# Spatial mixing of an attention and gMLP block in 26 block products instead of 28, on one Trainium2 core

## The chip, the cores and the metric

The kernel runs on one core of a Trainium2 chip. A core has five engines with queues of their own, which run in order and meet only at semaphores: TensorE (PE, matrix products, with its weight loads shown as PEld), VectorE (DVE), ScalarE (ACT), GpSimd (POOL) and SyncE (SP), which here only issues DMAs. SBUF is the working memory with 128 partitions, PSUM holds eight banks of 128 x 512 float32 into which TensorE accumulates. The metric is the device time in microseconds (us) of one execution; the median of several runs counts.

## What is computed

A block of a transformer with 2048 rows and 448 columns in float32: layer norm with a modulation from a condition vector, 16-head attention, then a second layer norm with modulation and a gated MLP whose gate mixes the rows. The part that the change touches most is the second half:

```python
z = _gelu(jnp.einsum("bsd,df->bsf", x, w_in))
z1 = z[..., :Fh]
z2 = _layernorm(z[..., Fh:], axis=-1)
g = jnp.einsum("ts,bsf->btf", w_sp, z2) + b_sp[None, :, None]
return jnp.einsum("bsf,fd->bsd", z1 * g, w_out)
```

Fh is 896, so g is the product of a 2048 x 2048 matrix w_sp with the 2048 x 896 matrix z2. This is the spatial mixing.

## The kernel before

Precision. TensorE works on float32r operands, a rounded float32. To come near float32 the kernel splits an operand into a high part (rounded) and a low part (the rest) and does three products: high by high, high by low, low by high. A split is a copy on ScalarE (`act.activation(hi, raw, AF.Copy)`) and a subtraction on VectorE (`sub`, line 82). So each 128 x 128 by 128 x 512 block costs three matmuls (lines 1262 to 1264, in `mix_step`) and needs both operands split.

Order of the work. The schedule is written by hand: instructions go to each engine's queue in program order. First the projections; then attention (lines 790 to 900), a loop over 256 slots, 16 to a head: per slot four score products (`s_mm`), four products for the running maximum (`m_mm`) of a head 20 slots ahead, and the value products (`pv_mm`). A table of events hangs further work on slots: at a head's slot of the maximum, `m_max` reduces on VectorE and then does three small operations on GpSimd, and `m_fin` transposes the result on TensorE and writes it by DMA into the query tile. Then the output projection, the first half of the gated MLP (`z1_unit`, stored to `z1_scr`), the second half (`z2_gemm` and `z2_norm`, 16 row tiles), the mixing, and the output product (`y_part`).

Sums of weight blocks. The mixing uses a fast matrix product in which blocks of w_sp are added or subtracted before they are multiplied. These sums depend on the weights only; they are made during attention. `ws_load(i)` fetches two 128 x 512 blocks into one of three pairs of buffers, `ws_add(i)` combines them on GpSimd (line 804), `ws_store(i)` writes the result to `ws_scr`. They sit on slots j, j + 3 and j + 5; there are 80 (five sums of 16 blocks) between slots 2 and 190. SP issues all these DMAs in order, so that a load waits until the store three sums before has landed.

Mixing. w_sp is cut into 2 x 2 blocks, z2 into two halves of rows and its first six channel tiles of 128 into two groups of three (`F1`, `F2`); the seventh tile (`F6`) is computed without the fast product along with them. That makes seven products of 2 x 2 block schemes, each four quarter-size blocks long: 28 block products of 2 x 4 by 4 x 4 blocks for the six tiles. They run in four phases of two halves of eight steps (`PHASES`, `steps`). A step loads the weight block or blocks (`w_load`), splits them (`w_split`), and does three matmuls for each of seven (last phase: four) channel tiles. At the end of each half `evac` adds seven accumulators into the four quarter results `u11` to `u22`. Sums of z2 for later phases are made on GpSimd (`z_sum`), the split stationary operands by `prep0` to `prep3`. `gate` adds the bias and multiplies by z1, `u_split` splits the result for the output product. The first four output tiles run inside the last phase, the other twelve behind it.

Of the kernel before, what the change touches and what calls it, by code (L numbers as in the profile page):

```python
# [31 lines left out]

@with_exitstack
def tile_adaln_mha_gmlp(ctx, tc, x, wqkv, wo, w_in, w_spT, b_sp, w_out, cT, w_mod0, w_mod, out):
# [13 lines left out]
    ws_scr = scr.tile([80, 128, 512], F32, name="ws_scr")  # L48
# [572 lines left out]
    ppool = att.enter_context(tc.tile_pool(name="ppool", bufs=6))  # L621

# [148 lines left out]
    def win_first(i):  # L771
# [6 lines left out]
    SUMS = (  # L778
        ((0, 1), (1, 1), ALU.subtract),
        ((1, 0), (0, 0), ALU.subtract),  # L780
        ((0, 0), (1, 1), ALU.add),
        ((0, 0), (0, 1), ALU.add),
        ((1, 0), (1, 1), ALU.add),
    )

    def w_block(rc, st, half):
        rb, cb = rc
        return w_spT[(rb * 8 + st) * 128 : (rb * 8 + st + 1) * 128, (2 * cb + half) * 512 : (2 * cb + half + 1) * 512]

    ws_raw = []  # L790

    def ws_tiles(i):
        if not ws_raw:
            ws_raw.append(dpool.tile([128, 7, 512], F32, name="ws_raw", tag="heapF"))
        return [ws_raw[0][:, 2 * (i % 3) + j, :] for j in range(2)]

    def ws_load(i):
        k, j = divmod(i, 16)
        for t, rc in zip(ws_tiles(i), SUMS[k]):
            sp.dma_start(t, w_block(rc, j // 2, j % 2))  # L800

    def ws_add(i):
        a, b = ws_tiles(i)
        pool.tensor_tensor(out=a, in0=a, in1=b, op=SUMS[i // 16][2])  # L804

    def ws_store(i):
        sp.dma_start(ws_scr[i], ws_tiles(i)[0])
# [315 lines left out]
    F1, F2, F6, FQ = slice(0, 384), slice(384, 768), slice(768, 896), slice(384, 896)  # L1123

    PHASES = (("s", 0, (1, 1)), ("s", 1, (0, 0)), ("s", 2, 3), ("s", 4, None))
    steps = [(p, half, st) for p in range(4) for half in range(2) for st in range(8)]

    def w_sources(p, half, st):
        _, k, q = PHASES[p]
        res = [ws_scr[k * 16 + st * 2 + half]]  # L1130
        if q is not None:
            res.append(ws_scr[q * 16 + st * 2 + half] if isinstance(q, int) else w_block(q, st, half))
        return res[::-1] if p == 3 else res
# [3 lines left out]
    def w_load(n):  # L1137
        if n < len(steps) and n not in raws and n not in wsp:
            raws[n] = []
            for src in w_sources(*steps[n]):  # L1140
                t = wp.tile([128, 512], F32, name="raw_sp")
                sp.dma_start(t, src)
                raws[n].append(t)

    def w_split(n):
        if n < len(steps) and n not in wsp:
            wsp[n] = []
            for raw in raws.pop(n):
                hi = wp.tile([128, 512], F32R, name="wsp_h")
                act.activation(hi, raw, AF.Copy)  # L1150
                lo = wp.tile([128, 512], F32R, name="wsp_l")
                sub(dve, lo, raw, hi)
                wsp[n].append((hi, lo))

    def z_sum(dst, a, b, op=ALU.add, eng=pool):
        eng.tensor_tensor(out=dst, in0=a, in1=b, op=op)

    def z_part(hi, lo, src):
        act.activation(hi, src, AF.Copy)
        sub(dve, lo, src, hi)  # L1160

    def prep0(st):
# [10 lines left out]
    def prep2(st):  # L1173
        z_part(zst[st][:, 0:896], zst[st][:, 896:1792], z2[st])
# [30 lines left out]
    for t in range(NT + 1):  # L1205
# [6 lines left out]
        if t in (13, 15):  # L1212
            w_split(t // 15)
# [305 lines left out]
```

## Time and profile before

| what | value |
|---|---|
| time, median of 3 runs | 1396.1 us (1394.71 to 1397.45) |
| the profiled execution: its time | 1395.53 us |
| the profiled execution: its span, first to last instruction | 1393.7 us |
| granted TensorE clock | 1.0 |
| attention, first score product to last value product | 145.1 to 866 us |
| z2 products | 977.9 to 1049.3 us |
| mixing with four output tiles | 1049.3 to 1336.9 us |
| remaining output tiles | 1336.9 us to the end |

How to read the lines below. In the groups of instructions a row gives the line of the kernel, engine, operation, output and inputs by the program's names, shapes, and the count; then total busy time and the mean duration of one in ns; then how long the engine was idle before them and what ended that wait. In the timeline a row begins with the start and the duration in us. Matmuls are pipelined, so that their durations overlap. A line can be that of a helper: line 82 is every subtraction of a split. "x12" behind a row counts the instructions merged into it.

### The profile page before, as it was taken

The page shows a single profiled execution, that of the slowest core. Times are in us where ns is not written, and L with a number is a line of the kernel's source. Part 1 is how long each engine was busy: PE and PEld are TensorE (multiplying, and loading weights), DVE is VectorE, ACT ScalarE, POOL GpSimd, SP SyncE. Part 2 cuts the span into 40 slices and gives each one's busy share as a digit, 9 for nine tenths or more (in the row PEclk, how much of TensorE's full clock was granted, in tenths as well). Part 3 has the DMA queues.
Part 4 walks back from the last instruction along what each step waited for, and adds up shares of the span by engine and source line. Part 5 has one row for each costly group of instructions (what it writes and reads, how often), then busy time and mean ns, then how long its engine had stood idle before and what let it go on. Part 6 is the DMA issues. An engine that isn't in the chain of part 4 may idle for free.

```text
span 1393.7 us, 20308 instructions
## 1 busy us (share of the span) xinstructions
PE 1388.7 (100%) x7170; PEld 987.0 (71%) x7170; DVE 1033.3 (74%) x1770; ACT 782.4 (56%) x1498; POOL 278.9 (20%) x279
## 2 busy tenths in 40 slices
PE   9999999999999999999999999999999999999998
PEld 8888655555555555555555555988998888888888
DVE  7898888888888888888888850850477655668574
ACT  6623677666667777777777779363234544434211
POOL 2144212222224143323200021100132330000000
PEclk9999999999999999999999999999999999999999
DMA  8465644655466556555323001534103333445453
GB/s 294 139 168 181 184 116 154 172 167 164 148 172 167 161 165 190 158 161 155 108 68 78 20 18 50 187 119 140 46 6 109 113 111 110 143 138 164 141 174 110
DMA packets 99633, 187.01 MB, mean 134 GB/s; under 512 B 17672, under 2 KB 29578, under 8 KB 96986
## 3 DMA queue, kind: packets, MB, share of 16 engines
q1 hardware_dynamic: 96814, 181.54, 43.2%
q10 hardware_dynamic: 2718, 4.19, 0.8%
q8 instruction: 56, 0.92, 0.3%
q14 instruction: 45, 0.37, 0.1%
HBM read 130.42 MB, written 50.46 MB: 130 GB/s over the span
## 4 chain that ended last, share of the span: by engine, by line
PE 99%; DVE 1%; DMA 0%; issue 0%; POOL 0%; ACTq 0%; DVEq 0%
PE st_ps L671 19%; PE o_ps L686 17%; PE mt L639 17%; PE acc L1262 7%; PE acc L1264 7%; PE acc L1263 7%; PE z_ps L1188 5%; PE pq L335 5%; PE z_ps L1074 5%; PE wo_ps L761 3%; PE pv L317 2%; PE y_ps L1369 2%; PE y_ps L1370 2%; PE y_ps L1368 2%; PE tp L111 1%; PE pv L464 0%
## 5 line engine op out<-in xcount | busy, mean ns | idle before, releaser
L644 DVE TENSOR_REDUCE pm<-mt 128x1 f32<-128x512 f32 x1024 | 631.0, 683 | 86.6 <-PE mt L639 86.6
L675 ACT ACTIVATE P<-st_ps 128x512 f32<-128x512 f32 x1024 | 516.4, 628 | 202.4 <-PE st_ps L671 201.6
L671 PE MATMUL st_ps<-qst,kst 128*128 128x512 f32 x1024 | 406.1, 406 | 0.0
L639 PE MATMUL mt<-kst,qst 128*128 128x512 f32 x1024 | 402.9, 393 | 0.0
L671 PEld LDWEIGHTS st_ps<-qst,kst 128*128 128x128 f32 x1024 | 191.1, 187 | 141.0 <-issue 93.1
L686 PE MATMUL o_ps<-P,V 128*32 128x512 f32 x2048 | 246.2, 598 | 0.0
L639 PEld LDWEIGHTS mt<-kst,qst 128*128 128x128 f32 x1024 | 192.4, 188 | 32.3
L804 POOL TENSOR_TENSOR ws_raw<-ws_raw 128x512 f32<-128x512 f32 x80 | 103.2, 1290 | 292.9 <-DMA ws_raw<-in_w_spT_dram 292.8
L1150 ACT ACTIVATE wsp_h<-raw_sp 128x512 fp32r<-128x512 f32 x112 | 70.2, 633 | 153.1 <-PE acc L1264 102.0
L82 DVE TENSOR_TENSOR wsp_l<-raw_sp,wsp_h 128x512 fp32r<-128x512 f32 x112 | 82.1, 742 | 81.1 <-ACT wsp_h L1150 80.4
L686 PEld LDWEIGHTS o_ps<-P,V 128*32 128x32 f32 x2048 | 53.5, 109 | 123.0 <-issue 117.7
L1262 PE MATMUL acc<-wsp_h,heapA 128*128 128x512 f32 x224 | 87.3, 390 | 0.0
L1263 PE MATMUL acc<-wsp_l,heapA 128*128 128x512 f32 x224 | 87.2, 389 | 0.0
L1264 PE MATMUL acc<-wsp_h,heapA 128*128 128x512 f32 x224 | 87.2, 389 | 0.0
L1263 PE MATMUL acc<-wsp_l,heapB 128*128 128x512 f32 x174 | 67.7, 389 | 0.0
L1264 PE MATMUL acc<-wsp_h,heapB 128*128 128x512 f32 x174 | 67.7, 389 | 0.0
L1262 PE MATMUL acc<-wsp_h,heapB 128*128 128x512 f32 x174 | 67.7, 389 | 0.0
L335 PE MATMUL pq<-heapD,heapD 128*128 128x512 f32 x196 | 61.9, 390 | 0.0
L1192 DVE BATCH_NORM_STATS2 stz<-z 128x6 f32<-128x448 f32 x32 | 19.8, 624 | 44.3 <-ACT z L1191 23.4
L1264 PEld LDWEIGHTS acc<-wsp_h,heapA 128*128 128x128 f32 x224 | 42.1, 188 | 8.8
L1262 PEld LDWEIGHTS acc<-wsp_h,heapA 128*128 128x128 f32 x224 | 42.0, 188 | 8.8 <-DVE cD L1268 0.3
L1263 PEld LDWEIGHTS acc<-wsp_l,heapA 128*128 128x128 f32 x224 | 42.1, 188 | 8.6
(225 smaller groups left out, 1600.5 us busy)
## 6 DMA issues: line engine op xcount, KB each, us to landing
ws_raw<-in_w_spT_dram SPq DMA_DIRECT2D x160, 256.0 KB
ws_scr<-ws_raw SPq DMA_DIRECT2D x80, 256.0 KB
raw_sp<-ws_scr SPq DMA_DIRECT2D x80, 256.0 KB
kst<-qk_scr SPq DMA_DIRECT2D x45, 224.0 KB
qst<-qk_scr SPq DMA_DIRECT2D x45, 224.0 KB
raw_sp<-in_w_spT_dram SPq DMA_DIRECT2D x32, 256.0 KB
qk_scr<-qh SPq DMA_DIRECT2D x28, 256.0 KB
qk_scr<-ql SPq DMA_DIRECT2D x28, 256.0 KB
```

Source lines behind the costliest of these rows:

```text
L82: eng.tensor_tensor(out=dst, in0=a, in1=hi.bitcast(F32), op=ALU.subtract)
L335: pe.matmul(pq, wqk[:, b, m * 128 : (m + 1) * 128], hT[g][:, a, :], start=j == 0, stop=j == NST - 1)
L639: pe.matmul(mt, qst[h % 3][:, t * 128 : (t + 1) * 128], kst[h % 3][:, kb * 512 : (kb + 1) * 512], start=True, stop=True)
L644: dve.tensor_reduce(out=pms[h][:, t, kb : kb + 1], in_=mt, axis=AX.X, op=ALU.max)
L671: pe.matmul(st, kst[h % 3][:, kt * 128 : (kt + 1) * 128], qst[h % 3][:, qb * 512 : (qb + 1) * 512], start=True, stop=True)
L675: act.activation(p, st, AF.Exp, scale=SCALE)
L686: pe.matmul(otile[h][32 * qb : 32 * qb + 32, :], V[:, kt, h, :], ptiles.pop((u, qb)), start=kt == 0, stop=kt == NT - 1)
L804: pool.tensor_tensor(out=a, in0=a, in1=b, op=SUMS[i // 16][2])
L1150: act.activation(hi, raw, AF.Copy)
L1262: pe.matmul(acc[i], zh, hi, start=st == 0, stop=False)
L1263: pe.matmul(acc[i], zh, lo, start=False, stop=False)
L1264: pe.matmul(acc[i], zl, hi, start=False, stop=st == 7)
```

## The change

The six channel tiles are now mixed in 26 block products. w_sp is used as a 4 x 4 arrangement of 512 x 512 blocks, z2 as 4 row groups by two channel groups. Each product p of `MIX` names the sums of z blocks to make first (`z_sum`, on GpSimd), the z operand and its sign, the weight operand (a stored sum, or a plain block), and which results take the accumulator's value after it. Two sets of three PSUM banks alternate between products, and they are never cleared: after product p the bank holds the sum over p, p - 2, p - 4 and so on, and `evac` adds or subtracts that running sum in the result.

In attention there are now 28 sums instead of five (each of four blocks, 112 sums of 128 x 512 instead of 80), some of sums made before; they take slots 2 to 243. For the 22 sums that are operands, two of four blocks also get their low part here, by a copy and a subtraction on GpSimd, and a second store to `wl_scr`. The mixing then loads these low parts in place of computing them; the other low parts of the 26 products are made on GpSimd.

Channel tile 6 is mixed in plain form: 64 block steps of three matmuls, spread over the steps of the products by `F6_AT` (12 of the 64 reuse a weight block that the product has loaded anyway). Its accumulator is one PSUM bank for a result at a time. The bias enters with the first eviction, so that `gate` is one operation. The four first output tiles run behind the mixing with the others. The reserved scratch for DMA descriptors is cut to 4096.

```diff
+W_SUMS = (
+    ((3, 3), (3, 1), -1),
...
+    (4, 11, -1),
...
+MIX = (
+    (((T0, 4, 7, 1), (T1, 0, T0, 1)), T1, 1, 6, ((1, 1, -1), (1, 3, -1))),
+    ((), T0, 1, 2, ((1, 0, 1),)),
+    (((ONCE, 3, T1, 1),), ONCE, 1, 3, ((0, 2, 1),)),
+    (((T1, 1, 2, 1), (ONCE, T1, T0, -1)), ONCE, 1, 11, ((0, 0, -1),)),
...
 def ws_add(i):
+    v, kt = divmod(i, 4)
     a, b = ws_tiles(i)
-    pool.tensor_tensor(out=a, in0=a, in1=b, op=SUMS[i // 16][2])
+    pool.tensor_tensor(out=a, in0=a, in1=b, op=ALU.add if W_SUMS[v][2] > 0 else ALU.subtract)
+    if v in W_OPERANDS and kt < 2:
+        hi = b.bitcast(F32R)
+        pool.tensor_copy(hi, a)
+        sub(pool, hi, a, hi)
 def ws_store(i):
-    sp.dma_start(ws_scr[i], ws_tiles(i)[0])
+    v, kt = divmod(i, 4)
+    a, b = ws_tiles(i)
+    sp.dma_start(ws_scr[i], a)
+    if v in W_OPERANDS and kt < 2:
+        sp.dma_start(wl_scr[2 * v + kt], b)
...
-    for i, slot in enumerate([j for j in range(2, 190, 2) if j % 16 != 12][:80]):
+    for i, slot in enumerate([j for j in range(2, 256, 2) if j % 32 != 28][: 4 * len(W_SUMS)]):
         at(slot, ws_load, i)
         at(slot + 3, ws_add, i)
         at(slot + 5, ws_store, i)
...
+    PARTS = {"h": (2048, 5), "l": (4608, 4), "p": (6144, 3)}
+    def z_sum(g):
+        for d, a, b, op in MIX[g // 4][0]:
+            if d == ONCE:
+                once[g] = wp.tile([128, 384], F32, name="once")
+            pool.tensor_tensor(
+                out=z_reg(d, g), in0=z_reg(a, g), in1=z_reg(b, g), op=ALU.add if op > 0 else ALU.subtract
+            )
+    def z_split(g):
+        _, r, sign, _, _ = MIX[g // 4]
+        src, (hi, lo) = z_reg(r, g), zs(g)
+        if sign > 0:
+            act.activation(hi, src, AF.Copy)
+            sub(dve, lo, src, hi)
...
+    def w_load(g):
+        v, kt = MIX[g // 4][3], g % 4
+        raws[g] = [wp.tile([128, 512], F32, name="raw_sp", bufs=5)]
+        if isinstance(v, int):
+            sp.dma_start(raws[g][0], ws_scr[4 * v + kt])
+            if kt < 2:
+                raws[g].append(w_part("p"))
+                sp.dma_start(raws[g][1].bitcast(F32), wl_scr[2 * v + kt])
+        else:
+            sp.dma_start(raws[g][0], w_block(*v, kt))
+        if g in F6_AT and not F6_AT[g][3]:
+            tb, k, kt, _ = F6_AT[g]
+            raws["f", g] = [wp.tile([128, 512], F32, name="raw_sp", bufs=5)]
+            sp.dma_start(raws["f", g][0], w_block(k, tb, kt))
+    def w_split(g):
+        for key, eng in ((g, pool), (("f", g), dve)):
+            if key in raws:
+                raw = raws.pop(key)
+                hi = w_part("h")
+                act.activation(hi, raw[0], AF.Copy)
+                if len(raw) == 1:
+                    raw.append(w_part("l"))
+                    sub(eng, raw[1], raw[0], hi)
+                wsp[key] = hi, raw[1]
...
     for t in range(NT + 1):
...
+        if 9 <= t < 13:
+            z_sum(t - 9)
+            b_load(bts(t - 9), t - 9)
+        if 10 <= t < 14:
+            z_split(t - 10)
+        if t >= 9:
+            z6_split(2 * t - 18)
+            z6_split(2 * t - 17)
+        if 11 <= t < 15:
+            w_load(t - 11)
         if t in (13, 15):
-            w_split(t // 15)
+            w_split((t - 13) // 2)
...
+    def mix_step(g):
+        p, kt = divmod(g, 4)
+        if p < 2 and kt == 0:
+            acc[p] = [bank("acc") for _ in range(3)]
+        zh, zl = zs(g)
+        hi, lo = wsp.pop(g)
         for f in range(3):
+            c, o = slice(f * 128, (f + 1) * 128), acc[p % 2][f]
+            pe.matmul(o, zh[:, c], hi, start=p < 2 and kt == 0, stop=False, skip_group_check=p > 1)
+            pe.matmul(o, zh[:, c], lo, start=False, stop=False, skip_group_check=p > 1)
+            pe.matmul(o, zl[:, c], hi, start=False, stop=kt == 3, skip_group_check=p > 1)
...
+    def evac(p, f):
+        for c, tb, sign in MIX[p][4]:
+            u = utile(3 * c + f, tb)
+            d_add(u, u if (c, tb) in started else bts(tb), acc[p % 2][f], ALU.add if sign > 0 else ALU.subtract)
...
+    for g in range(KS):
+        p, kt = divmod(g, 4)
+        w_load(g + 4)
+        w_split(g + 2)
+        z_split(g + 4)
+        if p and kt < 3:
+            evac(p - 1, kt)
+        z_sum(g + 6)
+        if g < 4:
+            b_load(utile(6, g), g)
+        if g + 2 in GATE_AT:
+            z1_load()
+        if g in GATE_AT:
+            gate()
+        if g >= 97:
+            u_split((6, 3, 4, 5, 0, 1, 2)[g - 97], 2)
...
+        mix_step(g)
...
-    nc = _bacc.Bacc("TRN2", target_bir_lowering=False, num_devices=1)
+    nc = _bacc.Bacc("TRN2", target_bir_lowering=False, num_devices=1, dynamic_dma_scratch_size=4096)
```

A step g is a quarter of a product: one of four row tiles, 9 matmuls, or 12 where channel tile 6 rides along. There are 104.

More of the change, by code (lines that the diff above doesn't have):

```diff
@@ L1135, in tile_adaln_mha_gmlp @@
-    raws, wsp = {}, {}
[L1137 to L1153, printed above, removed]
@@ L1360, in x2_load, with y_part @@
         sp.dma_start(x2t[t], x2_scr[t * 128 : (t + 1) * 128, :])
[L1362 removed]
+    def y_part(t, end=False):
         ts, uT = slice(t % 4 * 128, t % 4 * 128 + 128), uTs[t // 4]
[L1364 to L1375 removed]
@@ new lines, in y_part @@
+        o = x2t.pop(t)
+        for c, eng in ((slice(0, D), act),) if not end else ((slice(0, D // 2), act), (slice(D // 2, D), sp)):
+            dve.tensor_tensor(out=o[:, c], in0=o[:, c], in1=y[:, c], op=ALU.add)
+            eng.dma_start(out[t * 128 : (t + 1) * 128, c], o[:, c])
+    GATE_AT = (69, 70, 71, 76, 77, 79, 81, 83, 92, 93, 94, 95, 96, 97, 98, 99, 100)
+    WOUT_LOAD = (48, 49, 60, 61, 97, 99, 101)
+    WOUT_GATE = (50, 51, 62, 63, 98, 100, 102)
+    WOUT_PART = (51, 52, 63, 64, 100, 101, 103)
```

425 lines of the change are left out of this document (186 added, 239 removed).

## The prediction

> **What bounds the kernel now.** I read the page first: the engine totals, the slices and the chain of waits.
>
> ```profile
> span 1393.7 us, 20308 instructions
> PE 1388.7 (100%) x7170; PEld 987.0 (71%) x7170; DVE 1033.3 (74%) x1770; ACT 782.4 (56%) x1498; POOL 278.9 (20%) x279
> GB/s 294 139 168 181 184 116 154 172 167 164 148 172 167 161 165 190 158 161 155 108 68 78 20 18 50 187 119 140 46 6 109 113 111 110 143 138 164 141 174 110
> PE 99%; DVE 1%; DMA 0%; issue 0%; POOL 0%; ACTq 0%; DVEq 0%
> ```
>
> TensorE always has a matmul in flight, and 99% of the chain that ends last is TensorE. So the change gains only what it takes out of TensorE's own queue, and loses whatever it makes TensorE wait. The other engines matter as suppliers. The second view is the groups of instructions, for the spatial mixing (the lines 1262 to 1264 come alike):
>
> ```profile
> L1262 PE MATMUL acc<-wsp_h,heapA 128*128 128x512 f32 x224 | 87.3, 390 | 0.0
> L1262 PE MATMUL acc<-wsp_h,heapB 128*128 128x512 f32 x174 | 67.7, 389 | 0.0
> ```
>
> 224 + 174, and 2 more from z7l, are 400 at each of three lines: 1200 matmuls. Their 390 ns are no price, because matmuls overlap; the price is the distance from one start to the next, read from the third view, the timeline:
>
> ```profile
> 1049.27 0.39 PE L1262 MATMUL acc<-wsp_h,heapA 128*128 128x512 f32 x1
> ...
> 1331.70 0.36 PE L1368 MATMUL y_ps<-heapB,uT 128*128 128x448 f32 x1
> ...
> 1334.13 0.39 PE L1262 MATMUL acc<-wsp_h,heapB 128*128 128x512 f32 x1
> ...
> 1336.87 0.36 PE L1368 MATMUL y_ps<-heapB,uT 128*128 128x448 f32 x1
> ```
>
> From 1331.70 to 1334.13 run 12 output matmuls: 0.2025 us each. From 1334.13 to 1336.87 run 12 mixing matmuls: 0.228 us each. The whole stage, 1049.27 to 1336.87, is 287.6 us with 1200 mixing and 75 output matmuls (4 tiles of 21, less the last 9): (287.6 - 75 x 0.2025) / 1200 = 0.227 us. The stage has no visible gaps, so 0.227 us is my price.
>
> **What is removed from TensorE.** Before: three phases of 2 x 8 steps with 7 channel tiles and one with 4, three matmuls each: 3 x 336 + 192 = 1200. After: 26 products x 4 row tiles x 3 channel tiles x 3 = 936, and channel tile 6 in plain form, 64 x 3 = 192: 1128. That is 72 fewer, 72 x 0.227 = 16.3 us. The 336 output matmuls stay; the 84 of tiles 8 to 11 move from inside the last phase to behind the mixing, at the same price.
>
> **What is added around it, and its unit prices.**
>
> ```profile
> L82 DVE TENSOR_TENSOR wsp_l<-raw_sp,wsp_h 128x512 fp32r<-128x512 f32 x112 | 82.1, 742 | 81.1 <-ACT wsp_h L1150 80.4
> L82 DVE TENSOR_TENSOR heapA<-z,heapA 128x384 fp32r<-128x384 f32 x19 | 11.0, 595 | 0.0
> L1268 DVE TENSOR_TENSOR cE<-cE,acc 128x512 f32<-128x512 f32 x19 | 12.6, 684 | 1.0 <-PE acc L1264 1.0
> L1150 ACT ACTIVATE wsp_h<-raw_sp 128x512 fp32r<-128x512 f32 x112 | 70.2, 633 | 153.1 <-PE acc L1264 102.0 <-DVE x2t L1374 27.7 <-DMA raw_sp<-ws_scr 16.9
> L1159 ACT ACTIVATE heapA<-z 128x384 fp32r<-128x384 f32 x19 | 9.3, 512 | 0.0
> L804 POOL TENSOR_TENSOR ws_raw<-ws_raw 128x512 f32<-128x512 f32 x80 | 103.2, 1290 | 292.9 <-DMA ws_raw<-in_w_spT_dram 292.8
> L736 POOL CAST heapD<-heapD 128x512 fp32r<-128x512 f32 x12 | 7.3, 611 | 0.0
> ```
>
> A product is now 36 to 48 matmuls (12 where channel tile 6 rides along in a step, 9 where not): 8.2 to 10.9 us, 255.7 us in all. Against that:
> ScalarE: 156 weight halves x 0.633 + 104 stationaries x 0.512 = 152 us, 59%.
> VectorE: 52 low parts of channel tile 6 x 0.69 (the mean 0.742 holds waits; a free one takes 0.68, row below) + 104 stationaries x 0.595 + 108 evictions x 0.684 + 17 gates x 0.69 = 183 us, 72%. A product's evictions lie in the steps of the next product, and the banks they read are written again only by the one after that, 8 us or more later, so they are hidden; if VectorE lags by more, that product's first matmul waits.
> GpSimd: 60 low parts x 1.29 + 72 sums of z x 1.0 (row below) = 150 us, 58%.
> None is full by itself. What rows of before show as a joint limit is GpSimd with VectorE:
>
> ```profile
> L1156 POOL TENSOR_TENSOR z<-z,z x24: 1003/1260/4143, 1025.4 to 1131.9; 128x384 f32<-128x384 f32 x24
> ```
>
> That is one line's shortest, median and longest duration in ns; the timeline shows how they come about:
>
> ```profile
> 1058.81 0.68 DVE L82 TENSOR_TENSOR wsp_l<-raw_sp,wsp_h 128x512 fp32r<-128x512 f32 x1
> ...
> 1101.41 1.98 POOL L1156 TENSOR_TENSOR z<-z,z 128x384 f32<-128x384 f32 x2
> 1102.51 1.43 DVE L82 TENSOR_TENSOR wsp_l<-raw_sp,wsp_h 128x512 fp32r<-128x512 f32 x1 [1.94 <-ACT wsp_h L1150]
> ...
> 1106.45 2.44 POOL L1156 TENSOR_TENSOR z<-z,z 128x384 f32<-128x384 f32 x2
> ...
> 1106.61 0.64 ACT L1150 ACTIVATE wsp_h<-raw_sp 128x512 fp32r<-128x512 f32 x1 [2.08 <-PE acc L1264]
> ...
> 1111.37 0.64 ACT L1150 ACTIVATE wsp_h<-raw_sp 128x512 fp32r<-128x512 f32 x1 [2.08 <-PE acc L1264]
> ```
>
> A sum on GpSimd takes 1003 ns alone and up to 4143 ns. The VectorE subtraction at 1102.51 takes 1.43 us in place of 0.69: it ends 0.55 us after the GpSimd pair ends at 1103.39. They take turns. The changed mixing holds the shared resource for 150 us (GpSimd) + 52 x 0.69 + 104 x 0.595 + 17 x 0.69 = 109.5 us (VectorE, operands both in SBUF): 259 us of 255.7. By product, the sum exceeds TensorE's time in products 1, 2 (12.4 against 9.5 us), 8, 9, 13 to 17 and 19, 20, 22, 23 (worst: 13.7 against 9.5 in product 19); these excesses add up to 25 us. That is the upper bound of the loss. The lower bound is nothing: the last rows stand in a stretch where each step did 3 GpSimd sums (3.0 us alone) and 4 VectorE subtractions (2 x 0.69 + 2 x 0.595 = 2.57 us), 5.57 us of demand in 4.76 us from one ScalarE wait to the next, exactly 21 matmuls x 0.227, so no time was lost at 117%. A row's duration thus holds the resource for less than its length. Counting only demand above 117% of TensorE's time leaves 1.3 + 1.3 + 0.5 + 1.9 + 0.5 + 2.6 + 1.1 = 9 us; sums are issued six steps ahead, stationaries four, weight halves two (about 5 us), which swallows some. I take 4 us, nearer the stretch than the bound.
>
> [...]
>
> **The start of the mixing.**
>
> ```profile
> 1049.47 0.55 ACT L1191 ACTIVATE z<-z_ps 128x448 f32<-128x448 f32 x1 [1.69 <-PE z_ps L1188]
> ...
> 1050.03 1.14 DVE L1192 BATCH_NORM_STATS2 stz<-z 128x6 f32<-128x448 f32 x2
> ...
> 1051.45 0.15 DVE L101 TENSOR_SCALAR rsz<-mvz 128x1 f32<-128x1 f32 x1
> ...
> 1051.75 0.92 POOL L102 TENSOR_TENSOR rsz<-rsz,mhalf 128x1 f32<-128x1 f32 x1 [1.79 <-DVE rsz L101]
> ```
>
> The last z2 tile is normalised only after 1052.7. Now its split for channel tile 6 stands on ScalarE ahead of the weight half of step 2: 1052.7 + 0.7 (normalising) + 0.3 + 0.6 (half) + 1.3 (low part on GpSimd) = 1055.6, while step 2 is due at 1049.3 + 18 x 0.227 = 1053.4 and wants the low part 0.2 later. I take 2 us of stall; bounds 0 (VectorE's queue is shorter than before there) and 3.
>
> **Attention.** Its sums grow from 80 to 112, and 44 of them get a copy and a subtraction more: 112 x 1.29 + 44 x 1.9 = 228 us of GpSimd in place of 103.
>
> ```profile
> 409.53 0.22 DVE L651 TENSOR_REDUCE mxv<-pm 128x16 f32<-128x64 f32 x1
> 455.56 0.22 DVE L651 TENSOR_REDUCE mxv<-pm 128x16 f32<-128x64 f32 x1
> ...
> 731.79 0.22 DVE L651 TENSOR_REDUCE mxv<-pm 128x16 f32<-128x64 f32 x1
> 777.86 0.22 DVE L651 TENSOR_REDUCE mxv<-pm 128x16 f32<-128x64 f32 x1
> ...
> 450.00:600.00 150.00, 150.00 (x838) 86.64 (x836) 131.19 (x224) 105.19 (x210) 47.93 (x52) 1.00 0.57 167
> 750.00:820.00 70.00, 70.00 (x398) 40.30 (x393) 60.78 (x104) 48.71 (x97) 3.24 (x5) 1.00 0.19 46
> ```
>
> (The windows give busy time of TensorE, its weight loads, VectorE, ScalarE and GpSimd, the clock, DMA share and GB/s.) A head takes 46.03 us with GpSimd busy a third of the time and DMA at 0.57, and 46.07 us with both nearly idle (0.19). So this work costs the path nothing, and I cost more of it at nothing. [...] One place hangs on GpSimd: the running maximum.
>
> ```profile
> 317.48 0.22 DVE L651 TENSOR_REDUCE mxv<-pm 128x16 f32<-128x64 f32 x1
> ...
> 318.39 0.22 POOL L82 TENSOR_TENSOR mxp<-mxv,mxp 128x16 fp32r<-128x16 f32 x1
> ...
> 319.89 0.28 PE L660 MATMUL mtp<-ident,mxp 128*32 128x128 f32 x1
> ```
>
> GpSimd is done at 318.61, TensorE transposes at 319.89: 1.3 us of room. A sum of three operations (1.29 + 0.61 + 1.29 = 3.2 us) just ahead would stall TensorE by up to 1.9 us a head. But a sum is queued every second slot (5.8 us) and waits for its load, so it rarely lies right there; I take 0, bounds 0 and 14 heads x 1.9 x 44/112 = 10 us. SP's queue is passed by more DMAs; its waits (us in total, times, longest):
>
> ```profile
> SPq L800 <- DMA ws_scr<-ws_raw: 141.2, 54, 4.9
> ```
>
> A load waits for the store of three sums before (141.2 / 54 = 2.6 us), and behind it stand the maximum's row, the normalising chain and the next head's loads. A second store makes it some 3.5 us of each 5.8; the maximum's row is due four slots (11.5 us) later, so still covered; uncovered, each microsecond is TensorE's.
>
> **DMA in the mixing.**
>
> ```profile
> 1110.00:1180.00 70.00, 70.00 (x310) 57.98 (x309) 39.03 (x54) 29.77 (x50) 16.64 (x14) 1.00 0.36 110
> 1240.00:1300.00 60.00, 60.00 (x267) 49.67 (x266) 48.37 (x87) 26.17 (x52) 0.00 (x0) 1.00 0.49 158
> ```
>
> After: 104 + 52 blocks, 44 stored low parts and some 32 others of 262 KB are 61 MB in 255.7 us, 238 GB/s; the densest two products (16, 17) want 21 in 19.7 us, 279 GB/s. Shares of 0.36 at 110 and 0.49 at 158 scale to 305 and 322 GB/s when full, and the first slice moved 294. It fits, closely; I take 0, and the case where it doesn't is a rival.
>
> **End.** Output tiles 8 to 11 now follow the mixing, and VectorE's last four steps hold 3 evictions, a gate and 4 splits of 0.69 and 5 operations on w_out of some 0.62, 8.6 us in 8.2 us of matmuls. I take 0.5 us; bounds 0 and 1.5.
>
> **Sum.** The profiled execution took 1395.5 us (span 1393.7), 0.6 below the median. 1395.5 - 16.3 + 2 + 4 + 0.5 = 1385.7; on the median's scale 1386.3 us.
>
> **Rivals.**
> Full gain: the queues hide everything. For it: the 117% stretch without loss. Against: the start's chain is plain. 1396.1 - 16.3 = 1379.8.
> The shared resource becomes the bound: GpSimd and VectorE lag in products 1, 2, 13 to 17, 19 and 23, low parts come late, and TensorE waits for both. It decides when the 25 us of excess are paid in full rather than over 117%: 1379.8 + 2.5 + 25 = 1407. For it: 259 of 255.7 us, and a GpSimd operation of 4.1 us that got no turn. Against: the stretch above. This is the slower side.
> Attention gives it back: 1.9 us at the transposes weighted by 44/112, 10 us: 1386.3 + 10 = 1396, no change. For it: room of 1.3 us only. Against: GpSimd idles two thirds there.
> DMA becomes the bound: if no more than 220 GB/s is reached, 61 MB take 277 us, 21 more than TensorE: 1386.3 + 21 = 1407. For it: no stretch of the mixing moved over 174 GB/s. Against: those were not asked for more.
>
> **How the numbers follow.** Forecast 0.50, full gain 0.17, shared resource 0.14, attention 0.10, DMA 0.05, the rest unnamed. A change below 0.2% (2.8 us) can't be told from none. Faster (below 1393.3) is the forecast, the full gain, a tenth out of the partly paid rivals: 0.78. Same is mostly the attention case, 0.07; slower 0.15. The range 1379 to 1397 runs from the full gain to the attention case and leaves out the two slow rivals; the forecast's own is 1381 to 1392, since start, shared resource and end have the bounds 0 to 3, 0 to 9 and 0 to 1.5.
>
> **What would show it.** 1128 mixing matmuls 0.227 us apart; heads of 46.05 us as before; a gap of some 2 us at the mixing's third step; gaps behind GpSimd's low parts in products 1, 2, 16, 19 and 23, VectorE and GpSimd rows longer than alone. Wrong would be: heads over 46.3 us, DMA shares at 0.9 with TensorE waiting for loads, or evictions that slow beside GpSimd.

## The result and the profile after

The changed kernel takes 1415.2 us (median of four, 1414.19 to 1417.11) against 1395.5 us (four, 1394.71 to 1397.45): a ratio of 1.0141, 95% interval 1.0123 to 1.0158. It is 19.7 us slower where some 9 us less were forecast. The page of the changed kernel, the lines that answer to those of before:

```profile
span 1413.6 us, 20902 instructions
PE 1382.3 (98%) x7098; PEld 976.0 (69%) x7098; DVE 1086.3 (77%) x1788; ACT 816.7 (58%) x1578; POOL 535.8 (38%) x499
PE 7%; DVE 1%; issue 1%; DMA 1%; POOL 0%; ACT 0%; SPq 0%; DVEq 0%; ACTq 0%; POOLq 0%
```

There are 72 fewer matmuls, and yet the span grew: TensorE waits now. The chain's shares add up to a tenth only, so it says little; the stages, read from the first and last matmul of each in the timeline, say where:

| stretch, us | before | after |
|---|---|---|
| start to first score product | 145.1 | 146.9 |
| attention, first score product to last value product | 721.4 | 728.5 |
| from there to the MLP | 38.0 | 38.0 |
| MLP up to the mixing | 144.8 | 144.7 |
| mixing and output | 340.7 | 351.8 |

In the timeline of the mixing (first matmul, some of the longer waits with what ended them, first output matmul; line 147 of the changed kernel is the subtraction helper that was line 82, line 1300 the copy of a rounded part, line 1367 an addition, most often an eviction):

```profile
1058.09 0.39 PE L1380 MATMUL acc<-heapB,heapA 128*128 128x512 f32 x1
...
1064.09 0.50 PE L1381 MATMUL acc<-heapB,heapA 128*128 128x512 f32 x1 [0.85 <-POOL heapB L147]
...
1234.04 0.51 PE L1380 MATMUL acc<-heapB,heapA 128*128 128x512 f32 x1 [3.09 <-DVE cF L1367]
...
1263.45 0.50 PE L1381 MATMUL acc<-heapB,heapA 128*128 128x512 f32 x1 [3.47 <-DVE heapB L147]
...
1287.87 0.50 PE L1380 MATMUL acc<-heapB,heapA 128*128 128x512 f32 x1 [1.29 <-ACT heapB L1300]
...
1299.65 0.50 PE L1380 MATMUL acc<-heapB,heapA 128*128 128x512 f32 x1 [1.29 <-ACT heapB L1300]
...
1311.43 0.50 PE L1380 MATMUL acc<-heapB,heapA 128*128 128x512 f32 x1 [1.29 <-ACT heapB L1300]
...
1340.82 0.36 PE L1458 MATMUL y_ps<-wouts,uT 128*128 128x448 f32 x1
```

From 1058.09 to 1340.82 are 282.7 us, where 1128 x 0.2267 = 255.7 us was the price: 27.0 us of stall. The distances between matmuls, less 0.2267 us for each, place it in the steps (counting 9 or 12 matmuls to a step): 1.8 us in product 0, 8.6 in products 2, 14, 15 and 17, where an eviction is late (into `cD` or `cF`, line 1367), and 16.6 in products 19 to 23, at parts of weight tiles in `heapB`. The same 1.29 us at the same step of three products running (11.78 us apart) points to a fixed dependency rather than to a queue that lags. In the groups of instructions of the mixing VectorE's subtractions are slower than before, its evictions are not:

```profile
L147 DVE TENSOR_TENSOR heapB<-raw_sp,heapB 128x512 fp32r<-128x512 f32 x52 | 53.8, 1034 | 22.4 <-ACT heapB L1300 21.2 <-issue 1.0
L147 DVE TENSOR_TENSOR heapA<-z,heapA 128x384 fp32r<-128x384 f32 x44 | 41.6, 949 | 6.8 <-ACT heapA L1251 6.7
L1367 DVE TENSOR_TENSOR cD<-cD,acc 128x512 f32<-128x512 f32 x28 | 18.6, 675 | 0.0
```

1034 and 949 ns were 742 and 595; the eviction's 675 was 684. GpSimd's low part has a mean of 1424 ns on the page, where 1290 was the price. In attention, four of the distances from one head's transposition to the next are 46.7 to 47.3 us, the others, but for the first and the last, 46.0. In the timeline at the last head VectorE has the transposed maxima ready at 830.7, but SyncE issues their row only at 834.5, behind a store and two loads (the loads wait 3.4 us for a store to land):

```profile
829.76 0.38 SPq L870 DMA_DIRECT2D ws_scr<-ws_raw  x1
...
830.41 0.28 DVE L728 COPY nt<-mtp 32x128 f32<-32x128 f32 x1 [1.57 <-PE mtp L726]
...
833.60 0.81 SPq L856 DMA_DIRECT2D ws_raw<-in_w_spT_dram  x2
...
834.49 1.19 SPq L730 DMA_DIRECT2D qst<-nt  x2
...
837.95 1.51 PE L737 MATMUL st_ps<-qst,kst 128*128 128x512 f32 x4 [2.35 <-DMA qst<-nt]
```

So -16.3 (matmuls) + 27.0 (mixing) + 7.1 (attention) + 1.8 (ahead of attention) + 1.1 (output: 69.1 us for 336 x 0.2025) = 20.7, against 19.9 us of span.

### The profile page after: what moved, and what is told of

Same layout as the page of the kernel before. It is cut to its first block, busy times and chain, and to the rows that moved or that the text cites. A ratio compares the mean times of both kernels' runs of the same rounds, so it can differ in the third digit from the quotient of the medians.

```text
span 1413.6 us, 20902 instructions
## 1 busy us (share of the span) xinstructions
PE 1382.3 (98%) x7098; PEld 976.0 (69%) x7098; DVE 1086.3 (77%) x1788; ACT 816.7 (58%) x1578; POOL 535.8 (38%) x499
## 5 line engine op out<-in xcount | busy, mean ns | idle before, releaser
L861 POOL TENSOR_TENSOR ws_raw<-ws_raw 128x512 f32<-128x512 f32 x112 | 144.2, 1288 | 323.6 <-DMA ws_raw<-in_w_spT_dram 177.4
L1300 ACT ACTIVATE heapB<-raw_sp 128x512 fp32r<-128x512 f32 x156 | 97.5, 629 | 129.3 <-issue 41.9
L1380 PE MATMUL acc<-heapB,heapA 128*128 128x512 f32 x312 | 123.1, 395 | 11.3 <-ACT heapB L1300 5.6
L147 POOL TENSOR_TENSOR heapB<-raw_sp,heapB 128x512 fp32r<-128x512 f32 x60 | 85.2, 1424 | 109.4 <-ACT heapB L1300 91.1
L1382 PE MATMUL acc<-heapB,heapA 128*128 128x512 f32 x312 | 122.4, 392 | 0.0
L1381 PE MATMUL acc<-heapB,heapA 128*128 128x512 f32 x222 | 87.4, 394 | 8.4 <-DVE heapB L147 5.2
L1380 PEld LDWEIGHTS acc<-heapB,heapA 128*128 128x128 f32 x312 | 59.1, 190 | 27.4 <-ACT heapB L1300 7.7
L147 DVE TENSOR_TENSOR heapB<-raw_sp,heapB 128x512 fp32r<-128x512 f32 x52 | 53.8, 1034 | 22.4 <-ACT heapB L1300 21.2
L1382 PEld LDWEIGHTS acc<-heapB,heapA 128*128 128x128 f32 x312 | 59.0, 189 | 12.1
L147 POOL TENSOR_TENSOR ws_raw<-ws_raw 128x512 fp32r<-128x512 f32 x44 | 56.5, 1285 | 3.5
L167 POOL TENSOR_TENSOR rsz<-rsz,mhalf 128x1 f32<-128x1 f32 x16 | 14.6, 914 | 109.0 <-DMA tbuf<-in_b_sp_dram 64.7
L1381 PEld LDWEIGHTS acc<-heapB,heapA 128*128 128x128 f32 x222 | 41.8, 188 | 18.9 <-DVE heapB L147 6.1
```

What stands on the lines that cost most here:

```text
L147: eng.tensor_tensor(out=dst, in0=a, in1=hi.bitcast(F32), op=ALU.subtract)
L861: pool.tensor_tensor(out=a, in0=a, in1=b, op=ALU.add if W_SUMS[v][2] > 0 else ALU.subtract)
L1300: act.activation(hi, raw[0], AF.Copy)
L1380: pe.matmul(o, zh[:, c], hi, start=p < 2 and kt == 0, stop=False, skip_group_check=p > 1)
L1381: pe.matmul(o, zh[:, c], lo, start=False, stop=False, skip_group_check=p > 1)
L1382: pe.matmul(o, zl[:, c], hi, start=False, stop=kt == 3, skip_group_check=p > 1)
```

## The experiments

Attention and stall are read from each profiled execution, from ends rounded to 0.1 us; stall is the mixing's length less 255.7 us. The time is the median of two executions for most runs, so that it can lie some us from the profiled one. The kernel before took 1394.7 to 1396.2 us beside them. The first score product came at 145.0 to 148.8 us in kernels whose work up to there is the same, so the 1.8 us ahead of attention lie within what the same work varies by.

| run | time, us | attention | stall |
|---|---|---|---|
| after | 1415.2 | 728.5 | 27.0 |
| e1 attention alone | 1409.2 | 732.6 | - |
| e2 mixing alone | 1406.6 | 719.7 | 25.9 |
| e3 no sums of z | 1414.4 | 730.0 | 20.4 |
| e4 gates late | 1418.6 | 733.3 | 30.0 |
| e5 maxima on VectorE | 1420.7 | 731.6 | 30.5 |
| e6 e5 + other slots | 1410.5 | 724.6 | 27.6 |
| e7 eight raw tiles | 1419.4 | 732.4 | 30.8 |
| e8 channel tile 6 thinner | 1416.8 | 732.1 | 27.7 |
| e10 six rounded parts | 1408.7 | 728.7 | 20.4 |
| e11 six of either part | 1405.8 | 729.2 | 13.9 |
| e12 seven sums a head | 1416.7 | 720.9 | 29.5 |
| e13 e11 + e12, evictions first | 1403.2 | 721.0 | 15.8 |
| e14 eight sums a head | 1448.6 | 754.8 | 30.2 |
| e15 e11 + e14, evictions early | 1436.5 | 758.3 | 16.3 |
| e16 e15 without that | 1436.8 | 758.6 | 14.8 |
| e17 e11 + e12, last sums in the MLP | 1395.1 | 719.7 | 14.6 |
| e18 e17, six evictions early | 1396.7 | 721.3 | 15.6 |
| e19 e17, no sums of z | 1382.4 | 720.7 | 1.8 |

### Which half costs what

> The kernel before with the changed attention work alone: 112 sums of weight blocks, their low parts, their stores and issue slots; the mixing stays that of before and reads the first 80 stored blocks, so its values are others. Theory 1 (the longer GpSimd and SyncE work in attention delays the transposes of some heads and the row of the last one): attention ends 5 to 9 us later than before, 1401 to 1404 us. Rival (attention hides it as I forecast, and the 8.8 us that the trace shows there come from one execution): 1395 to 1397 us, heads all 46.0 us apart.

> The changed kernel with the attention work of before: 80 sums, no low parts made there; the mixing loads as many tiles as in the changed kernel, from the 80 stored ones, so its values are others. Theory 1 (attention and mixing each pay for themselves): the mixing still stalls 27 us, attention is as before: 1405 to 1408 us. Rival (attention was one execution's mishap): 1413 to 1416 us. If the mixing's stalls came from attention's later end they would go: about 1380 us, which I do not expect.

Both halves cost by themselves. In the eight profiled executions with the change's own attention (after, e1, e3, e4, e7, e8, e10, e11) it took 728.5 to 733.3 us, 7 to 12 more than before. e1 lies above its range: attention took 11 us more, and its first score product came 3.7 us later. e2, 1406.6 us, is as theory 1 had it, with attention at 719.7.

### The late stalls: which ring?

> The changed kernel with 21 of the 28 gates (product with z1, whose tiles take slots of the raw ring) moved behind the last product, two to an output tile. Theory B (z1 tiles in the ring of five make the weight loads of products 19 to 23 late): of their 16.6 us of stall 10 or more go, the tail gains at most 4 us: 1401 to 1409 us. Theory A (SBUF shared with GpSimd): the gates are VectorE operations with two SBUF inputs, 0.6 to 1 us each, in the same stretch, so part goes too, but the late stalls by heapB written by GpSimd stay: 1408 to 1413 us. Neither: 1413 to 1419 us.

```diff
-    GATE_AT = (69, 70, 71, 76, 77, 79, 81, 83, 92, 93, 94, 95, 96, 97, 98, 99, 100)
+    GATE_AT = (69, 70, 71, 76, 77, 79, 81)
```

> The changed kernel with eight raw tiles in the ring in place of five (the ring of parts of z has six slots instead of eight, twelve of the rounded z tiles of channel tile 6 lie in the room that this frees). Theory B (loads of products 19 to 23 start late for want of a free raw tile): their 17 us of stall shrink to 4 or less: 1400 to 1404 us. Theory A alone (VectorE late through GpSimd at SBUF): they stay above 10 us: 1408 to 1416 us. The stalls of products 2, 15 and 17 (8 us) stay in either case.

```diff
-        raws[g] = [wp.tile([128, 512], F32, name="raw_sp", bufs=5)]
+        raws[g] = [wp.tile([128, 512], F32, name="raw_sp", bufs=8)]
```

> The changed kernel with the twelve tiles of channel tile 6 and token block 3 spread thinner: every second step of 80 to 94 and steps 100 to 103, in place of three of four steps of 80 to 95. Theory B (1.75 raw tiles per step are more than a ring of five carries): the stalls of products 20 to 23 (10.8 us) fall to 3 or less, product 19's (5.8) stays, product 25 may stall 1 to 2: 1405 to 1410 us. Rival (each of these stalls is VectorE's or ScalarE's own queue): 1412 to 1416 us.

```diff
-        (3, [g for g in range(80, 96) if g % 4 != 3], 24),
+        (3, [*range(80, 96, 2), *range(100, 104)], 24),
```

Theory B falls by the steps: with eight raw tiles (e7) the stalls of products 19 to 23 stay, at steps 84, 88 and 92 to 0.02 us. e4 says less, because it moves only the gates from step 83 on; those of steps 76 to 81 stay in the mixing. Its late stalls stay as well. Thinner work (e8) moved the stalls instead: those of steps 84, 88 and 92 went, and two came at steps 100 and 101, where four steps running now have a tile more. The times of e7 and e8 lie 1 to 3 us above every range on record; their attention took 732 us. Two rows of e8's timeline:

```profile
1329.74 0.80 PE L1380 MATMUL acc<-heapB,heapA 128*128 128x512 f32 x1 [5.61 <-ACT heapB L1300]
...
1335.50 0.50 PE L1380 MATMUL acc<-heapB,heapA 128*128 128x512 f32 x1 [1.29 <-ACT heapB L1300]
```

That fits the other rings, `PARTS`: five slots for rounded parts (`h`), four for remainders (`l`), the low parts. `w_split(g + 2)` stands ahead of `mix_step(g)`, so the parts of three steps are held, six where each has a tile of channel tile 6. Counted through the program, a slot is rewritten ahead of its reader at steps 78, 79, 80, 81, 84, 88 and 92, and with e8's steps at 78, 80, 100 and 101: just where the stalls are. There the matmuls of the changed kernel read the part of a tile of two steps later, and TensorE waits until that has been made. So this is a fault of the change and not only a delay: at these seven steps the kernel as measured multiplies by parts of other tiles. Larger rings give these steps their own parts again (the same count finds no such step in e11, e13 and e15 to e19).

> The changed kernel with six slots instead of five for the rounded parts of weight tiles (the parts of z keep six slots of eight, which makes the room). Theory B2: step g issues the split of step g+2 ahead of its own matmuls, so the parts of three steps are held at once; counted through the program, the ring of five is overrun at steps 80, 84, 88 and 92 (the part of tile 86 goes into the slot that step 84 still has to read), the ring of four remainders at 78, 79, 80 and 81, and TensorE then waits for the later tile's copy. These are just the steps with late stalls. Six slots for the rounded parts alone: the four stalls of 1.44 us at 80, 84, 88 and 92 go, those of 78, 79, 81 and the second of 80 (8 us) stay: 1408 to 1411 us. Rival (the raw ring or VectorE's queue): 1414 to 1418 us.

> As the run with six slots for the rounded parts, and six instead of four for the remainders. Theory B2: no slot is rewritten before it is read, all 17 us of stall at steps 78 to 92 go, 1397 to 1401 us; those of products 2, 15 and 17 stay. Rival (loads or queues are as late as the parts, and only take over the wait): 1404 us or more.

```diff
-    PARTS = {"h": (2048, 5), "l": (4608, 4), "p": (6144, 3)}
+    PARTS = {"h": (2048, 6), "l": (4608, 6), "p": (6144, 3)}
+    MORE = {("h", 5): 0, ("l", 4): 1, ("l", 5): 2}
```

(e10 has 6 and 4.) Theory B2 holds step by step: in e10 the waits of 1.29 us at 80, 84, 88 and 92 are gone, those at 78, 79 and 81 stay; in e11 all are gone. e11's time, 1405.8 us, lies above B2's range and in that of its rival (1404 or more). The stall fell by 13.1 us and not by 17, since evictions that the late stalls had covered took 3.5 us in their place, and the output took 1.8 us more; so the rival has a small part in it: VectorE's queue took over 3.5 us, and no load did. All of e11's waits above 1.5 us in the mixing's timeline:

```profile
1081.22 0.50 PE L1384 MATMUL acc<-heapB,heapA 128*128 128x512 f32 x1 [1.93 <-DVE cD L1371]
...
1212.17 0.50 PE L1384 MATMUL acc<-heapB,heapA 128*128 128x512 f32 x1 [2.14 <-DVE cD L1371]
...
1234.45 0.68 PE L1384 MATMUL acc<-heapB,heapA 128*128 128x512 f32 x1 [2.26 <-DVE cF L1371]
...
1278.87 0.50 PE L1384 MATMUL acc<-heapB,heapA 128*128 128x512 f32 x1 [1.82 <-DVE cE L1371]
```

### Attention: queues or load?

> The changed kernel with the three small operations on each head's row maxima (negation, rounded part, remainder) on VectorE instead of GpSimd. Theory 1 (the transposes of the maxima wait behind two sums with their low parts, 3.2 us each, in GpSimd's queue): the waits for mxp (0.6 to 3.2 us in two to four heads of each run so far) go, 2 to 6 us less: 1409 to 1413 us; the wait of the last head for its row, 1.8 to 2.7 us, stays. Rival (VectorE, busy 87% of attention, takes longer for the maxima, or the row's transfer is what is late): 1414 to 1418 us.

```diff
-        pool.tensor_scalar(out=mx, in0=mx, scalar1=-1.0, scalar2=None, op0=ALU.mult)
+        dve.tensor_scalar(out=mx, in0=mx, scalar1=-1.0, scalar2=None, op0=ALU.mult)
```

> As the run with the maxima's operations on VectorE, and the sums of weight blocks issued in other slots: the slot in which a head's row is written is left free in 14 of 16 heads (before: in all, changed kernel: in half), the last sums come correspondingly later. Theory 1 (SyncE's queue, with loads and one or two stores per sum, makes the row late): the waits for the row go too, attention within 2 us of before, 1406 to 1410 us. Rival (the row waits for the DMA engines, not for the queue, or the later sums hurt the last heads): same as the run with VectorE alone, 1409 to 1416 us.

> The changed kernel with the 112 sums of weight blocks issued in other slots from the third head on: seven of sixteen, so that none adds just ahead of a head's maxima and none loads or stores in the slot in which its row is written; the maxima stay on GpSimd. Theory D (order in GpSimd's and SyncE's queues): attention within 2 us of before: 1405 to 1409 us. Rival (the transfers or GpSimd's load as such): attention stays 6 us or more late: 1412 to 1418 us.

```diff
-[j for j in range(2, 256, 2) if j % 32 != 28][: 4 * len(W_SUMS)]
+[j for j in range(251) if (j % 2 == 0 if j < 32 else j % 16 in (1, 2, 4, 6, 9, 13, 15))]
```

Maxima on VectorE (e5, above both its ranges) only passed the wait on: score products waited 0.56 us for a reduction, and 1.54 and 2.68 us for rows. Other slots on top of that (e6: every even one but the seventh of a head) took 7.0 us off attention, though not all of its loss; at 1410.5 us it lies just above its theory's range. With the maxima on GpSimd again, e12 has attention back at 720.9 us. But its sums run to slot 249, and 6.7 us turn up behind the last head, so that its time is in its rival's range. In its timeline, SyncE's queue, the sum that it waits for, and TensorE:

```profile
863.54 0.94 SPq L856 DMA_DIRECT2D ws_raw<-in_w_spT_dram  x2
864.59 5.45 SPq L870 DMA_DIRECT2D ws_scr<-ws_raw  x2
...
868.12 1.57 POOL L861 TENSOR_TENSOR ws_raw<-ws_raw 128x512 f32<-128x512 f32 x1 [8.56 <-DMA ws_raw<-in_w_spT_dram]
...
873.88 9.37 SPq L792 DMA_DIRECT2D heapD<-osb  x5
...
884.23 2.21 PE L827 MATMUL wo_ps<-heapD,heapD 128*128 128x448 f32 x5 [5.03 <-DVE heapD L147]
```

A store waits 4.6 us for a sum, and that for its load; behind the store two loads of `x` wait for it to land (1.9 us), and the last head's results queue behind these.

> Six slots for either kind of part, the slots of the run before for the sums, and the evictions issued ahead of the splits in each step. If the three causes are what I hold them to be: attention +2, mixing 16.3 less than before plus 2 at its start and up to 5 in products 2, 15 and 17: 1382 to 1390 us, faster than both kernels. If the evictions cannot be brought forward, since VectorE is late as a whole: 1388 to 1393 us. If one of the three fails, 1395 us or more.

> The changed kernel with the 112 sums issued eight to a head in the first fourteen heads, in slots whose sums end before a head's maxima and whose stores and loads leave the slot of its row free. Theory D (only the order in GpSimd's and SyncE's queues costs attention its time): heads 46.0 us apart, output projection 41 us as before, 1405 to 1409 us. Rival (112 sums with low parts cannot be hidden, wherever they stand): the heads with eight sums take 46.5 us or more, 1411 us or more.

```diff
+[j for j in range(224) if j % 16 in (1, 3, 5, 6, 9, 10, 13, 15)]
```

e13 (with `evac` ahead of `w_split`) ends in the same way, at 1403 us and not at the 1382 to 1390 expected. e14 is the worst miss: eight sums a head end early enough, but from the fourth head on a head takes 46.6 to 51.9 us. Its timeline at one of them:

```profile
419.15 0.28 DVE L728 COPY nt<-mtp 32x128 f32<-32x128 f32 x1 [0.87 <-PE mtp L726]
...
420.88 0.37 SPq L870 DMA_DIRECT2D ws_scr<-ws_raw  x1
...
424.44 1.29 POOL L861 TENSOR_TENSOR ws_raw<-ws_raw 128x512 f32<-128x512 f32 x1 [5.67 <-DMA ws_raw<-ws_scr]
...
424.96 0.33 SPq L856 DMA_DIRECT2D ws_raw<-in_w_spT_dram  x1
425.35 0.42 SPq L856 DMA_DIRECT2D ws_raw<-ws_scr  x1
425.87 0.38 SPq L870 DMA_DIRECT2D ws_scr<-ws_raw  x1
426.34 1.19 SPq L730 DMA_DIRECT2D qst<-nt  x2
...
430.33 0.47 PE L737 MATMUL st_ps<-qst,kst 128*128 128x512 f32 x1 [3.65 <-DMA qst<-nt]
```

The row is ready at 419.4 and issued at 426.3. SyncE stands 3.7 us between a store and the next load, 3.6 of them until a store has landed. GpSimd waits 5.67 us for a load in the same stretch, and the store just ahead of the row is issued when GpSimd's sum is done, at 425.7: each waits in order for another. Leaving the row's slot free is no help when the queue ahead of it runs late. Whether it is the eighth sum or the closer spacing was not told apart.

> The changed kernel with six slots for either kind of part, 104 of the 112 sums in attention (eight in each of the first two heads, then seven, none ahead of a head's maxima or in the slot of its row, the last in slot 230), the last eight sums during the second GEMM of the MLP, and the split of step 2 before the mixing. Theory: attention and output projection as before the change (904 to 905 us at its end), second GEMM unhindered, mixing 12 to 14 us of stall left in products 2 to 25: 1391 to 1395 us, at or just under the kernel before. If eight sums beside the second GEMM hold it up, or the heads still wait for their rows: 1397 us or more.

```diff
+        if t < 8:
+            wz[104 + t] = [wp.tile([128, 512], F32, name="wz", tag="raw_sp", bufs=5) for _ in range(2)]
+            ws_load(104 + t)
```

With 104 sums in attention, seven a head from the third head on, and eight in the second GEMM, attention takes 719.7 us and nothing is late behind it. (The split of step 2 is also issued ahead of the mixing here; the 1.8 us of stall at step 2 stay.) The kernel is level with the one before: 1395.05 against 1394.99 us, ratio 1.0009 (0.9999 to 1.0018). No version that does the whole work beats the kernel before.

### The rest: GpSimd beside VectorE

> The changed kernel without the GpSimd sums of z in products 1 to 25 (the first operand is used in place of the sum, and the running sums stay as the first product leaves them). Theory A (GpSimd and VectorE wait for each other at SBUF, so evictions and low parts come late): the stalls of products 2, 15, 17 (8.4 us) and half or more of those of 19 and 20 (11.8 us) go: 1399 to 1406 us. [...]

```diff
+            if g >= 4:
+                if d == ONCE:
+                    once[g] = z_reg(a, g)
+                continue
```

> Those slots, six slots for either kind of part, and the evictions of the second and third channel tile both in the product's second step. If the evictions only came a step late: products 2, 15, 17 and 21 lose 3 us or less in place of 11, 1383 to 1389 us. If VectorE beside GpSimd is too slow as a whole: the stalls only turn up elsewhere, at remainders or evictions, 10 us or more in all, 1390 to 1394 us.

> As the run before with the evictions where the changed kernel has them: 12 to 14 us of stall in products 0, 2, 15, 17 and 21 as with the larger rings alone, 1391 to 1396 us.

```diff
-        if p and kt < 3:
-            evac(p - 1, kt)
+        for f in ((0,), (1, 2), (), ())[kt] if p else ():
+            evac(p - 1, f)
```

> As the run before, with the third channel tile's eviction one step earlier in six products only (those whose eviction TensorE waits for at the start of products 2, 15, 17, 21, 22 and 23), and the split of step 2 in the last but one turn of the second GEMM. If it is order: 10 us or more of the 14.6 us of stall go, 1383 to 1388 us, faster than the kernel before. If VectorE is short of time beside GpSimd: the stalls turn up one to four steps later at remainders, 8 us or more stay, 1389 to 1394 us.

In e3 the stalls of products 15 and 17 went and those of 19 to 23 stayed, at 17.8 us: two causes. (Its two executions took 1409.4 and 1419.4 us, so only the steps of the profiled one, the faster, are read.) Evictions a step earlier, in all products (e15 against e16) or in six (e18 against e17), took the waits away where they were and brought as many elsewhere, at remainders made by GpSimd among others: 16.3 against 14.8 and 15.6 against 14.6 us. So moving evictions ahead in VectorE's queue does not help. (e14's slots put e15 and e16 more than 40 us above their ranges; only their stalls are compared.)

> The run with the last eight sums in the second GEMM, without GpSimd's 64 sums of z in the mixing from product 1 on (the first operand is used in place of the sum, and the running sums stay as the first product leaves them). If GpSimd's sums beside VectorE are what makes evictions late: of the 14.6 us of stall 9 or more go, leaving step 2 (1.7) and some of product 2: 1382 to 1388 us. If VectorE is short of time by its own work: 10 us or more stay, 1391 to 1395 us.

Without the sums 1.8 us of stall are left, those of step 2, and the time is 1382.4 us, ratio 0.991 (0.9894 to 0.9927); it leaves out work that the result needs, so it is no kernel to use. The sums cause the other 12.8 us of e17's stall. VectorE's groups in e19's mixing:

```profile
L147 DVE TENSOR_TENSOR heapA<-z,heapA 128x384 fp32r<-128x384 f32 x72 | 51.2, 712 | 9.4 <-ACT heapA L1263 9.3
L1386 DVE TENSOR_TENSOR cD<-cD,acc 128x512 f32<-128x512 f32 x27 | 17.9, 675 | 0.0
```

The subtraction takes 712 ns in place of 949 in the changed kernel, the eviction 675 as there. From 1200 to 1300 us the subtraction for the parts of z takes 1039 ns in e17 and 731 in e19, that for a weight tile 977 and 810, the eviction 674 and 675: beside the sums the subtractions are longer, the evictions are not.

Another way for the sums to cause the stall would be that VectorE, which works in order, stands waiting for what a late sum delays. The traces speak against it. VectorE ahead of e17's longest wait for an eviction (2.25 us, at 1225.99), and at the same work in e19:

```profile
1221.79 1.40 DVE L147 TENSOR_TENSOR heapA<-raw_sp,heapA 128x512 fp32r<-128x512 f32 x1
1223.11 1.63 DVE L1263 SCALAR_TENSOR_TENSOR heapA<-once,heapA 128x384 fp32r<-128x384 f32 x1
1224.66 0.67 DVE L1382 TENSOR_TENSOR cC<-cC,acc 128x512 f32<-128x512 f32 x1
...
1211.83 0.68 DVE L147 TENSOR_TENSOR heapA<-raw_sp,heapA 128x512 fp32r<-128x512 f32 x1
1212.43 0.54 DVE L1267 SCALAR_TENSOR_TENSOR heapA<-z,heapA 128x384 fp32r<-128x384 f32 x1
1212.90 0.67 DVE L1386 TENSOR_TENSOR cC<-cC,acc 128x512 f32<-128x512 f32 x1
```

In e17 VectorE does not stand still there from 1211.8 to the eviction at 1225.3: the two operations shown take 1.40 us against 0.68 in e19 and 1.63 against 0.54, and the evictions, 0.67 us in both, come late behind them. Over the whole mixing VectorE is busy 235.6 of 270.3 us in e17 and 199.1 of 257.5 us in e19.

## Why the prediction was wrong, step by step

**Matmuls, -16.3 us: right.** 1128 at 0.2267 us are what e19's mixing shows (257.5 us with 1.8 of stall).

**Start of the mixing, 2 us: right**, 1.8 in nearly every run, and at the third step.

**GpSimd with VectorE, 4 us: the right cause, too small.** It is 8.6 us in the changed kernel and 12.8 with mended rings (e17: 14.6 less 1.8), between my 4 and the 25 of the bound. Two steps failed. The 117% that the old stretch bore without loss was carried over to a mixing in which VectorE also evicts all the time; VectorE's own sum, 183 us, was priced without any stretching (and without the work on w_out and the last splits); in e17 it was busy 235.6 us. And the evictions were called hidden by "8 us or more": that holds for the first channel tile (four steps), but the third's eviction is issued two steps after the first's, and its bank is written again two steps and six matmuls later, 24 to 30 x 0.2267 = 5.4 to 6.8 us. The waits came at evictions more than at low parts. That the joint demand of 259 us takes in, of VectorE's operations, those with both operands in SBUF alone was the author's estimate, which no run shows as a rule: from 1200 to 1300 us the means in e17 and e19 are 1039 and 731 ns for the subtraction for the parts of z and 674 and 675 for the eviction, but 0.88 and 0.86 us for the gates, which that sum takes in too.

**Attention, 0: wrong; its rival of 10 us was right in size, but not in path.** The runs show 7 to 12 us. The rival put all of it at the transpositions. In the changed kernel's profiled execution 1.9 us are waits at three transpositions and 2.8 at two rows, in e8's 5.0 and 4.0 at three each; the rest of the 7.1 us was not traced. I said that a sum rarely lies just ahead of the maxima, and that the row of the maxima is due 11.5 us later and so covered. The second was misread from the start. In the kernel before, the row is ready at 780.84, and the head's first score product, which reads it, starts at 788.00:

```profile
780.56 0.28 DVE L662 COPY nt<-mtp 32x128 f32<-32x128 f32 x1
...
780.87 1.19 SPq L664 DMA_DIRECT2D qst<-nt  x2
...
788.00 0.39 PE L671 MATMUL st_ps<-qst,kst 128*128 128x512 f32 x1
```

That is 7.2 us and not 11.5, and 4.8 at the last head. A row that is waited for takes 3.5 us from its issue to the product (834.49 to 837.95 above), so a queue that lags by 3 to 4 us is enough to make TensorE wait, and by 1.3 us at the last head. There the row was issued 3.8 us late. Both kinds of wait are waits in order: in e14 the row stood 6.9 us in SyncE's queue behind a load that waited for a store to land and a store whose sum waited for its load. I took the mean wait of a store and not the chain. VectorE's reductions in attention were not slowed by GpSimd's longer work there: 682 ns in the kernel before, 681 in the changed one.

**What was not in the prediction at all: the part rings, 16.6 us.** It is the largest error. e11 takes these stalls away, with a net gain of 13.1 us of stall. I priced each engine's work, SyncE's queue and the transfers, and never counted how many slots three steps need, which put this term at nothing without a reason. With attention's 7.1 us it turns the forecast of 1386 into a loss.

**DMA, 0: held.** The stalls went in e19 with every transfer of the mixing still there. **End, 0.5:** 1.1.

## What to carry to other kernels

Before a schedule that works ahead is costed, count for each ring of buffers how many tiles are alive between their writing and their reading, step by step; with the ring one slot short TensorE waited here 1.29 us for later work at the same step of three products running. A table of slots says when work is issued, not when a queue gets to it: follow store, operation and load through the in-order queue to what stands behind them, and read from a trace how much room that has (a head's row had 7.2 us in the kernel before; in e14 one stood 6.9 us in the queue). Where a trace shows operations of one engine longer beside another's, as VectorE's subtraction here (949 ns, 712 without the sums in e19), price them at the longer time and add up the whole queue, with the evictions that stand in it.

## What the runs showed of the hardware

Behind one wait of 3.09 us, at 1234.04, TensorE ran at about half its pace. The timeline of the changed kernel has

```profile
1235.52 0.63 PE L1392 MATMUL acc<-heapB,z6h 128*128 128x512 f32 x1
1235.95 0.63 PE L1393 MATMUL acc<-heapB 128*128 128x512 f32 x1
1236.37 0.63 PE L1380 MATMUL acc<-heapB,heapA 128*128 128x512 f32 x1
...
1238.03 0.39 PE L1381 MATMUL acc<-heapA 128*128 128x512 f32 x1
1238.26 0.39 PE L1382 MATMUL acc<-heapB,heapA 128*128 128x512 f32 x1
```

and its windows

```profile
1234.00:1238.00 4.00, 3.96 (x10) 3.13 (x11) 3.54 (x6) 1.67 (x3) 2.64 (x3) 0.57 0.48 138
1263.00:1267.00 4.00, 3.01 (x12) 2.17 (x12) 2.15 (x5) 1.35 (x3) 0.65 (x1) 1.00 0.56 197
```

Matmuls come 0.43 us apart in place of 0.23 until about 1238, at a granted clock of 0.57, which cost 1.7 us on top of the wait. Behind the longer wait of 3.47 us at 1263.45 the clock stayed at 1.00. At the same step of product 17 a wait of 3.09 us in e2 was followed by a clock of 1.00 over the next 4 us, and one of 3.10 us in e4 by 0.50. So the length of the wait does not decide here by itself; what does was not shown.
